# Selective attention with a top-1 expert layer: the router's logits and ranks moved to the end of a slot, one batch's logits in four column groups, ranks in two products, block ends by transfers

## The chip, the cores and the metric

The kernel runs on one core of a Trainium2 chip. The metric is the device time of one launch in microseconds (us); the median of three runs is compared. A core has five engines with instruction queues of their own: TensorE (PE; its weight loads are shown apart, as PEld), VectorE (DVE), ScalarE (ACT), GpSimd (POOL) and SyncE (SP), which here only issues transfers. Each runs its queue in order and waits on semaphores. A matmul takes a stationary operand from SBUF (the weight load) and streams a moving operand through the array into PSUM.[...]

## The reference, cut to what matters

Eight batches, eight heads, 576 tokens, 64 channels per head; then eight experts with a hidden size of 1024. All fp32.

```python
scores = scale * q @ k^T + min(-(cum[i] - cum[j]), 0)   # cum: running sum of max(s, 0); causal
attn   = softmax(scores)                                # divided by (sum + 1e-9)
x      = attn @ v                                       # (B, S, 512), heads side by side
logits = x @ w_gate                                     # eight columns
local  = sigmoid(x @ w_local)                           # one column
for b, s in order:
    fresh = argmax(logits[b, s])
    e = fresh if s == 0 or local[b, s] < 0.5 else prev_e
    prev_e = e
    p = softmax(logits[b, s])
    out[b, s] = p[e] * (relu(x[b, s] @ w1[e]) @ w2[e])
```

A token either takes its own best expert or that of the token before it, so the choice is a running scan along each batch. Tokens are then sorted by expert, so that an expert's weights meet many tokens at once.

## The kernel before

**Attention** goes in slots. There are 32 pairs (eight batches, four head pairs each), and slot n computes the scores of pair n and the values of pair n-1. In PE order a slot is: `scores` in four units (L884; 384, 2 x 192, 448 and 320 + 64 columns, each for two heads side by side in the row halves of the array), then the first block of `values` (L909, query blocks 0 to 5: 48 records in the trace), then the second block (query blocks 6 to 8: 52 records). An fp32 matmul leaves two records. Behind each block DVE takes the block out of PSUM (L915, L916), and behind the second it transposes the pair's rows into `xt` (L927, function `turn`). ACT computes the exponentials of the scores (L885), POOL masks the diagonal blocks (L870), DVE multiplies the values of a later batch by key weights (L856, `weigh`).

The rest is planned by hand into places of slots with `plan(slot, place, f)`: place 0 lies between the second and the third score unit, place 1 between the two value blocks, place 3 behind the second block, `turn` and the slot's `weigh`. What is planned into a place is issued there in the order of the `plan` calls, on whichever engines it uses.

**Router.** The eight batches make four groups of two. A group's stages are `product` (PE: x times the 9 gate columns, kept as 32 columns, into the PSUM tile `lp`; the moving operand is `xt`), `logits` (DVE: a 32 x 32 transpose `lt` and copies into `l`), `codes`, `turn1`, `turn2` (DVE: the scan over tokens, ending in the one-hot `hot` and its running count `incl`), `ranks` (PE: sums of `incl` and `hot` over partitions into the PSUM tile `pos`), `rows` (DVE: each token's row in a table in HBM), `gates` (DVE, with an index ramp by POOL: the weight p[e] beside each token) and 18 calls of `scatter` (POOL issues an indirect transfer of 128 half rows to the table). For the first three groups they lie in slots n+1 to n+12, with n = 8, 16 and 24. The last group's batches are done one by one: the product of the first in slot 29, that of the second inside the first expert unit, followed by its `codes` to `turn2`; its `ranks`, `rows`, `gates` and scatters follow there.

**PSUM.** Two banks hold the two value blocks. The other six are three tiles of two banks with one tag, `banks(name)`: each score unit takes one, and so do `lp`, `pos` and `wep`. A new tile must wait for the readers of the tile that held its banks: ACT for scores, DVE for `lp` and `pos`, ACT for `wep`.

**Single buffers.** `xt` of the even and of the odd batch of a group have one buffer each. The `turn` of the first pair of the next even batch therefore waits until the product of the group before has read it.

**Block ends.** `range_ends` and `range_ends_sum` spread the key weights at each block's end over 128 partitions into `wend`, by a mask, a selection matrix and a matmul (`wep`, L843). `wend` is read much later, in the expert phase, by a check of value ranges.

**Experts.** Work is cut into units; unit 0 starts right behind the last values. `fetch` (SP) reads a unit's rows from the table; it waits for all scatters issued before it in program order. `turn_x` (DVE) transposes them, `layer1` and `layer2` are the matmuls (L569, L593). Scatters that found no place in a slot are issued one by one between the chunks of `layer1`, and when the list of these is empty in unit 0 the units 2 and 3 are fetched. The weights of an expert are 2 MB per layer; those of the first load come in four parts, planned at place 3 of slots 25 to 28.

Of the kernel before, what the change touches and what calls it, by code (L numbers as in the profile page):

```python
# [9 lines left out]
F32 = mybir.dt.float32  # L10
# [99 lines left out]
class Router:  # L110
# [8 lines left out]
    def constants(self):  # L119
# [29 lines left out]
        self.seg = self.t("seg", [P, E, NC])  # L149
        nc.gpsimd.memset(self.seg, 1.0)  # L150
        nc.gpsimd.memset(self.seg[:, :, 0:1], 0.0)
        self.first = self.t("first", [P, P])
# [37 lines left out]

    def product(self, g, xts, banks, bs=range(GB)):

        ps = self.g.setdefault(g, {})["lp"] = banks("lp")[:, 0, : NJH * 32]
        i = 0
        for hp in range(HP):
            for d in range(2):
                for b in bs:
                    for c in range(2):
                        at = 32 * (2 * b + c)
                        j = c * (NJ - NJH)  # L200
                        self.nc.tensor.matmul(ps[at : at + 32], lhsT=self.wx[:, hp, d],  # L201
                                              rhs=xts[b][:, hp, d, j : j + NJH].rearrange("p j t -> p (j t)"),
                                              start=(i == 0), stop=(i == 2 * HP - 1))
                i += 1

    def logits(self, g, bs=range(GB)):
        v = self.nc.vector
        st = self.g[g]
        p = slice(DH * bs[0], DH * bs[-1] + DH)
        lt = self.s("lt", [P, NJH, 2, WR])  # L210
        v.transpose(lt[p].rearrange("p j q e -> p (j q e)"), st.pop("lp")[p])
        if "l" not in st:
            st["l"] = self.s("l", [P, NC, E + 1])
        l = st["l"]
        for b in bs:
            for c in range(2):
                j = b * NJ + c * NJH
                skip = c * (2 * NJH - NJ)
                for r in range(2):
                    at = 32 * (2 * b + c)  # L220
                    v.tensor_copy(l[32 * r : 32 * r + 32, j : j + NJH - skip],
                                  lt[at : at + 32, skip:, r, : E + 1])
        c = slice(bs[0] * NJ, bs[-1] * NJ + NJ)
        v.tensor_copy(l[DH:, c], l[:DH, c])
# [35 lines left out]
    def turn2(self, g):  # L260
        v = self.nc.vector
        st = self.g[g]
        for a in range(4):
# [12 lines left out]
        hot = st["hot"] = self.s("hot", deep)  # L276
        v.tensor_tensor(hot, e.unsqueeze(1).to_broadcast(deep), self.eidx.unsqueeze(2).to_broadcast(deep),
                        op=Alu.is_equal)
        incl = st["incl"] = self.s("incl", deep)
        v.tensor_tensor_scan(incl.rearrange("p e c -> p (e c)"), self.seg.rearrange("p e c -> p (e c)"),  # L280
                             hot.rearrange("p e c -> p (e c)"), 0.0, op0=Alu.mult, op1=Alu.add)

    def ranks(self, g, banks):
# [3 lines left out]
        n = E * NC  # L287
        ps = st["pos"] = banks("pos")[:, 0, : n + E]
        mm(ps[:, n:], lhsT=self.first, rhs=incl[:, :, NC - 1], start=True, stop=True)  # L289
        mm(ps[:, :n], lhsT=self.first, rhs=incl.rearrange("p e c -> p (e c)"), start=True, stop=False)  # L290
        mm(ps[:, :n], lhsT=self.later, rhs=st["hot"].rearrange("p e c -> p (e c)"), start=False, stop=True)

    def rows(self, g):
        v = self.nc.vector
        st = self.g[g]
        pos = st.pop("pos")
        n, deep = E * NC, [P, E, NC]
        at = self.s("at", deep)
        v.tensor_tensor(at, pos[:, :n].rearrange("p (e c) -> p e c", e=E), self.base.unsqueeze(2).to_broadcast(deep),
                        op=Alu.add)  # L300
        v.tensor_tensor(self.base, self.base, pos[:, n:], op=Alu.add)
        v.tensor_tensor(at, at, st["hot"], op=Alu.mult)
# [5 lines left out]
    def gates(self, g, xb):  # L308
# [3 lines left out]
        ex, hot = st.pop("ex"), st.pop("hot")  # L312
# [411 lines left out]
def attention(ctx, tc, q, k, vm, vt, s, wx, ident, recs, wend, router, experts):  # L724
# [97 lines left out]
    mask_ends = []  # L822

    def range_ends():
        mask = once.tile([B * H, NPAIR], F32, name="mask")
        nc.gpsimd.tensor_tensor(mask, ident[: B * H, :NPAIR], ident[: B * H, NPAIR : 2 * NPAIR], op=Alu.add)
        ends = once.tile([B * H, NPAIR, NJ], F32, name="ends")
        for w, a, z in ((w1, 0, 2 * G1), (w2, 2 * G1, NJ)):
            shape = [B * H, NPAIR, z - a]
            nc.vector.tensor_tensor(ends[:, :, a:z], mask.unsqueeze(2).to_broadcast(shape),  # L830
                                    w[:, a * DH + DH - 1 : z * DH : DH].unsqueeze(1).to_broadcast(shape), op=Alu.mult)
        sel = once.tile([B * H, 2, DH], F32, name="sel")
        nc.gpsimd.memset(sel, 1.0)
        nc.gpsimd.affine_select(out=sel[:, 0], in_=sel[:, 0], compare_op=Alu.is_ge, fill=0.0, base=NPAIR - 1,
                                pattern=[[0, DH]], channel_multiplier=-1)
        nc.gpsimd.affine_select(out=sel[:, 1], in_=sel[:, 1], compare_op=Alu.is_ge, fill=0.0, base=-NPAIR,
                                pattern=[[0, DH]], channel_multiplier=1)
        mask_ends.extend((sel, ends))

    def range_ends_sum():  # L840
        sel, ends = mask_ends
        wp = banks("wep")[:, 0, : NPAIR * NJ]
        mm(wp, lhsT=sel.rearrange("p h d -> p (h d)"), rhs=ends.rearrange("p n j -> p (n j)"), start=True, stop=True)  # L843
# [754 lines left out]
```

## Time and profile before

| what | us |
|---|---|
| median of three runs (752.2 to 753.45) | 752.59 |
| the profiled execution, own time | 744.71 |
| its span, first to last instruction | 743.0 |
| of it: PE busy from 7 to 218 us (attention, 211 us) | 206.81 |
| of it: PE busy from 218 to 736 us (experts, 518 us) | 518.00 |
| of it: PE busy from 736 to 743 us (last store) | 0.24 |

The granted TensorE clock is 0.998 of full speed over the span. The three PE rows come from the view that sums busy time over stretches. The profiled execution is 7.9 us shorter than the median of the timed runs; a difference between two kernels is worked out in the profiled execution's own time and then taken from the median.

The views used below are: the page's busy line and its chain of waits in shares; the chain in order of time (start, length, engine, tile, line, number of records); the groups of instructions by line and form; the waits by engine; and the timeline of one engine.

### The profile page before, as it was taken

What the parts mean: (1) busy time and instruction counts of PE and PEld (TensorE: products, weight loads), DVE (VectorE), ACT (ScalarE), POOL (GpSimd) and SP (SyncE); (2) the same over time, 40 slices, a digit from 0 to 9 for tenths busy, and PEclk for the clock granted to TensorE, in tenths of its full rate; (3) what the DMA queues carried; (4) which work ended last, traced back from release to release, by engine and by line L of the source; (5) the groups of instructions that cost most, each with busy time, mean ns of one, the idle gap of its engine ahead of it and who ended that gap; (6) DMA issues with size and microseconds to landing.
All of it is one profiled execution on the core that took longest, in us unless ns stands there. A gap on an engine that the chain in (4) does not pass through costs nothing.

```text
span 743.0 us, 15903 instructions
## 1 busy us (share of the span) xinstructions
PE 730.5 (98%) x6455; PEld 501.7 (68%) x6455; DVE 246.4 (33%) x647; ACT 162.2 (22%) x319; POOL 211.2 (28%) x453
## 2 busy tenths in 40 slices
PE   8999999999999999999999999999999999999996
PEld 5888888888786757757756376546745576647674
DVE  4655846866663741100110511230041001050110
ACT  4554544454331101101102010101100011101110
POOL 2653396686573435420110101010101001010110
PEclk9999999999999999999999999999999999999999
DMA  6672474667758958689447969996999955899000
GB/s 206 234 246 87 143 228 138 197 219 232 237 215 345 326 188 287 263 341 282 154 153 247 375 242 426 308 390 240 420 329 368 425 197 225 286 404 337 29 15 34
DMA packets 55285, 186.09 MB, mean 250 GB/s; under 512 B 11549, under 2 KB 32285, under 8 KB 46880
## 3 DMA queue, kind: packets, MB, share of 16 engines
q1 hardware_dynamic: 48400, 164.86, 62.5%
q0 software_dynamic: 6800, 20.09, 7.1%
q8 instruction: 53, 0.87, 0.5%
q14 instruction: 32, 0.26, 0.1%
HBM read 164.31 MB, written 20.88 MB: 249 GB/s over the span
## 4 chain that ended last, share of the span: by engine, by line
PE 94%; DVE 3%; POOL 0%; issue 0%; POOLq 0%
PE yp L593 35%; PE hp L569 31%; PE po L909 12%; PE ps L884 11%; PE hp L560 4%; PE lp L201 2%; DVE xb L916 0%; DVE ei L264 0%; DVE xt L927 0%; DVE recs L915 0%; POOL table L338 0%; DVE incl L280 0%; PE pos L290 0%; PE pos L289 0%; POOL e L870 0%
## 5 line engine op out<-in xcount | busy, mean ns | idle before, releaser
L593 PE MATMUL yp<-w2b,hT 128*128 128x512 f32 (+2 forms) x752 | 259.3, 594 | 0.0
L569 PE MATMUL hp<-xT,w1b 128*128 128x256 f32 (+1 forms) x1216 | 233.2, 352 | 0.0
L569 PEld LDWEIGHTS hp<-xT,w1b 128*128 128x128 f32 x1216 | 206.4, 191 | 32.5 <-issue 7.8
L593 PEld LDWEIGHTS yp<-w2b,hT 128*128 128x128 f32 (+2 forms) x752 | 108.1, 167 | 140.8 <-issue 139.5
L598 POOL DMA_INDIRECT out_dram<-y,gi x37 | 36.1, 975 | 420.4 <-DVE y L596 391.8
L571 ACT ACTIVATE hT<-hp 128x256 f32<-128x256 f32 (+1 forms) x152 | 54.0, 355 | 429.6 <-PE hp L569 429.6
L596 DVE TENSOR_SCALAR y<-yp,gi 128x512 f32<-128x512 f32 x37 | 27.6, 746 | 309.1 <-PE yp L593 302.7
L885 ACT ACTIVATE e<-ps 128x768 f32<-128x768 f32 (+1 forms) x128 | 97.1, 836 | 99.4 <-PE ps L884 99.3
L909 PE MATMUL po<-vg,e 128*64 128x66 f32 x3200 | 102.7, 224 | 1.6 <-POOL e L870 0.9
L909 PEld LDWEIGHTS po<-vg,e 128*64 128x64 f32 x3200 | 96.8, 138 | 6.1 <-POOL e L870 2.0
L884 PE MATMUL ps<-qb,kb 64*128 64x192 f32 (+4 forms) x768 | 97.5, 400 | 0.2 <-ACT e L885 0.2
L884 PEld LDWEIGHTS ps<-qb,kb 64*128 64x128 f32 x768 | 67.7, 187 | 28.6 <-ACT e L885 9.2
L338 POOL DMA_INDIRECT table<-xb,idx x72 | 73.8, 1025 | 22.3 <-issue 20.4
L870 POOL TENSOR_SCALAR_AFFINE_SELECT e<-e 128x256 f32<-128x256 f32 (+1 forms) x160 | 65.9, 438 | 45.5 <-ACT e L885 44.7
L580 DVE STREAM_TRANSPOSE hT<-hs 32x256 f32<-32x256 f32 x64 | 27.9, 436 | 74.8 <-ACT hs L562 74.0
L856 DVE TENSOR_TENSOR vg<-va,wk 128x1024 f32<-128x1024 f32 (+1 forms) x21 | 29.8, 1417 | 6.7 <-DMA va<-in_vm_dram 6.6
L916 DVE TENSOR_TENSOR xb<-po,recs 128x384 f32<-128x384 f32 x64 | 29.3, 458 | 3.0 <-DVE recs L915 0.7
L915 DVE RECIPROCAL recs<-po 128x12 f32<-128x12 f32 x64 | 13.3, 207 | 47.1 <-PE po L909 47.1
L539 DVE STREAM_TRANSPOSE xT<-xq 128x1024 f32<-128x1024 f32 (+1 forms) x23 | 23.6, 1028 | 14.9 <-DMA xq<-table 14.6
L560 PE MATMUL hp<-w1b,xT 128*32 128x512 f32 (+1 forms) x224 | 28.3, 594 | 0.0
L927 DVE STREAM_TRANSPOSE xt<-xb 128x576 f32<-128x576 f32 x32 | 24.9, 778 | 1.1
L560 PEld LDWEIGHTS hp<-w1b,xT 128*32 128x32 f32 (+1 forms) x224 | 8.2, 114 | 17.7 <-issue 17.5
(230 smaller groups left out, 171.0 us busy)
## 6 DMA issues: line engine op xcount, KB each, us to landing
w1b<-in_w_dram SPq DMA_DIRECT2D x29, 2048.0 KB, 8.2
w2b<-in_w_dram SPq DMA_DIRECT2D x29, 2048.0 KB, 15.1
kb<-in_k_dram SPq DMA_DIRECT2D x32, 288.0 KB, 3.8
qb<-in_q_dram SPq DMA_DIRECT2D x32, 288.0 KB, 3.4
xq<-table SPq DMA_DIRECT2D x56, 130.0 KB, 12.1
va<-in_vm_dram SPq DMA_DIRECT2D x7, 1024.0 KB, 7.0
w1b<-in_w_dram SPq DMA_DIRECT2D x4, 512.0 KB, 6.2
w2b<-in_w_dram SPq DMA_DIRECT2D x4, 512.0 KB
```

What stands on the lines that cost most here:

```text
L338: put = self.nc.gpsimd.indirect_dma_start(out=self.halves, in_=src, element_offset=0, in_offset=None, out_offset=bass.IndirectOffsetOnAxis ...
L560: mm(ps[d, :], lhsT=xT[:, k, d], rhs=self.ws[l][0][:, k, c * 512 : c * 512 + 512], start=(k == 0), stop=(k == DK - 1))
L569: mm(ps[:, :w], lhsT=self.ws[ls[0]][0][:, k, c * P : c * P + P], rhs=xT[:, k, :w], start=(k == 0), stop=(k == DK - 1))
L571: nc.scalar.activation(self.hT[u][:, c, :w], ps[:, :w], Act.Relu)
L593: mm(ps[d, :], lhsT=hT[:, k, n * P + d.start : n * P + d.stop], rhs=self.ws[l][1][:, k, :], start=(k == 0), stop=(k == FK - 1))
L598: put = nc.gpsimd.indirect_dma_start(out=self.out[:, :], out_offset=bass.IndirectOffsetOnAxis(ap=gi.bitcast(I32)[:, n, 0:1], axis=0), in_= ...
L856: nc.vector.tensor_tensor(vgs[b % 2][g][:, c0:c1].rearrange("p c h e -> p (c h) e")[:, :, :DH], va[:, c0:c1].rearrange("p c h e -> p (c h) ...
L870: nc.gpsimd.affine_select(out=ap, in_=ap, compare_op=Alu.is_ge, fill=0.0, base=base, pattern=n, channel_multiplier=-1)
L884: mm(ps[:, h, at : at + z - a], lhsT=kb[d, key : key + P], rhs=qb[d, a:z], start=True, stop=True)
L885: nc.scalar.activation(e, ps, Act.Exp, scale=scale)
L909: mm(po[d, j - j0, :], lhsT=weights_of(n, c, j, h), rhs=vg[:, c, 2 * hp + h, :], start=(c == 0), stop=(c == last))
L916: nc.vector.tensor_tensor(xb[:, j0:j1, :, 32 * hp : 32 * hp + 32], po[:, :, :DH].rearrange("p j (g i) -> p j g i", g=2), rec[:, :, 0].unsq ...
```

## The change

- `product` of a group of two batches keeps its four column groups; `product` of a single batch (twice, in the last group) uses four column groups of three token blocks (96 columns) where it used two of five (160 columns). The blocks of neighbouring groups overlap, and the copies of `logits` skip the overlap.
- `product` and `logits` go from place 1 to place 3 of their slot; `ranks` and `rows` from place 1 to place 3; `gates` from place 1 of slot n+4 to place 1 of slot n+5. The scatters begin at place 1 of slot n+5, where they began at place 3 of n+4, and place 0 is used in slots n+6 to n+8. The fetch of units 0 and 1 moves one slot on.
- `hot` becomes one constant tile with a 19th column of zeros for each expert; `incl` and `seg` are widened to match. Column 19 of `pos` then is the group's total, and the separate product for the totals goes.
- `range_ends` copies the block ends with POOL to a [64, 9] tile, stores it in HBM and loads it back as two broadcasts; the mask, the selection matrix, the product `wep` and ACT's copy go.

```diff
@@ -146,9 +146,11 @@
         for p in (0, DH):
             for b in range(GB):
                 nc.gpsimd.memset(self.thr[p : p + 1, b * NJ : b * NJ + 1], -1e30)
-        self.seg = self.t("seg", [P, E, NC])
+        self.seg = self.t("seg", [P, E, NC + 1])
         nc.gpsimd.memset(self.seg, 1.0)
         nc.gpsimd.memset(self.seg[:, :, 0:1], 0.0)
+        self.hot = self.t("hot", [P, E, NC + 1])
+        nc.gpsimd.memset(self.hot, 0.0)
         self.first = self.t("first", [P, P])
         nc.gpsimd.memset(self.first[:DH], 1.0)
         nc.gpsimd.memset(self.first[DH:], 0.0)
@@ -188,38 +190,38 @@
     def s(self, name, shape, dt=F32, **kw):
         return self.sb.tile(shape, dt, name=name, **kw)
 
+    @staticmethod
+    def columns(bs):
+
+        if len(bs) == 2:
+            return NJH, [(b, j, j // (NJ - NJH)) for b in bs for j in (0, NJ - NJH)]
+        return 3, [(bs[0], j, min(j, 1)) for j in range(0, NJ - 2, 2)]
+
     def product(self, g, xts, banks, bs=range(GB)):
 
-        ps = self.g.setdefault(g, {})["lp"] = banks("lp")[:, 0, : NJH * 32]
-        i = 0
-        for hp in range(HP):
-            for d in range(2):
-                for b in bs:
-                    for c in range(2):
-                        at = 32 * (2 * b + c)
-                        j = c * (NJ - NJH)
-                        self.nc.tensor.matmul(ps[at : at + 32], lhsT=self.wx[:, hp, d],
-                                              rhs=xts[b][:, hp, d, j : j + NJH].rearrange("p j t -> p (j t)"),
-                                              start=(i == 0), stop=(i == 2 * HP - 1))
-                i += 1
+        n, groups = self.columns(bs)
+        ps = self.g.setdefault(g, {})["lp"] = banks("lp")[:, 0, : n * 32]
+        last = HP * 2 - 1
+        for i in range(HP * 2):
+            hp, d = divmod(i, 2)
+            for c, (b, j, _) in enumerate(groups):
+                self.nc.tensor.matmul(ps[32 * c : 32 * c + 32], lhsT=self.wx[:, hp, d],
+                                      rhs=xts[b][:, hp, d, j : j + n].rearrange("p j t -> p (j t)"),
+                                      start=(i == 0), stop=(i == last))
 
     def logits(self, g, bs=range(GB)):
         v = self.nc.vector
         st = self.g[g]
-        p = slice(DH * bs[0], DH * bs[-1] + DH)
+        n, groups = self.columns(bs)
         lt = self.s("lt", [P, NJH, 2, WR])
-        v.transpose(lt[p].rearrange("p j q e -> p (j q e)"), st.pop("lp")[p])
+        v.transpose(lt[:, :n].rearrange("p j q e -> p (j q e)"), st.pop("lp"))
         if "l" not in st:
             st["l"] = self.s("l", [P, NC, E + 1])
         l = st["l"]
-        for b in bs:
-            for c in range(2):
-                j = b * NJ + c * NJH
-                skip = c * (2 * NJH - NJ)
-                for r in range(2):
-                    at = 32 * (2 * b + c)
-                    v.tensor_copy(l[32 * r : 32 * r + 32, j : j + NJH - skip],
-                                  lt[at : at + 32, skip:, r, : E + 1])
+        for c, (b, j, skip) in enumerate(groups):
+            for r in range(2):
+                v.tensor_copy(l[32 * r : 32 * r + 32, b * NJ + j + skip : b * NJ + j + n],
+                              lt[32 * c : 32 * c + 32, skip:n, r, : E + 1])
         c = slice(bs[0] * NJ, bs[-1] * NJ + NJ)
         v.tensor_copy(l[DH:, c], l[:DH, c])
 
@@ -273,33 +275,30 @@
         v.tensor_scalar(e, cf[:, :NC], -1.0, None, Alu.add)
         v.tensor_scalar(e, e, E - 1, None, Alu.bitwise_and)
         deep = [P, E, NC]
-        hot = st["hot"] = self.s("hot", deep)
-        v.tensor_tensor(hot, e.unsqueeze(1).to_broadcast(deep), self.eidx.unsqueeze(2).to_broadcast(deep),
-                        op=Alu.is_equal)
-        incl = st["incl"] = self.s("incl", deep)
+        v.tensor_tensor(self.hot[:, :, :NC], e.unsqueeze(1).to_broadcast(deep),
+                        self.eidx.unsqueeze(2).to_broadcast(deep), op=Alu.is_equal)
+        incl = st["incl"] = self.s("incl", [P, E, NC + 1])
         v.tensor_tensor_scan(incl.rearrange("p e c -> p (e c)"), self.seg.rearrange("p e c -> p (e c)"),
-                             hot.rearrange("p e c -> p (e c)"), 0.0, op0=Alu.mult, op1=Alu.add)
+                             self.hot.rearrange("p e c -> p (e c)"), 0.0, op0=Alu.mult, op1=Alu.add)
 
     def ranks(self, g, banks):
         mm = self.nc.tensor.matmul
         st = self.g[g]
         incl = st.pop("incl")
-        n = E * NC
-        ps = st["pos"] = banks("pos")[:, 0, : n + E]
-        mm(ps[:, n:], lhsT=self.first, rhs=incl[:, :, NC - 1], start=True, stop=True)
-        mm(ps[:, :n], lhsT=self.first, rhs=incl.rearrange("p e c -> p (e c)"), start=True, stop=False)
-        mm(ps[:, :n], lhsT=self.later, rhs=st["hot"].rearrange("p e c -> p (e c)"), start=False, stop=True)
+        ps = st["pos"] = banks("pos")[:, 0, : E * (NC + 1)]
+        mm(ps, lhsT=self.first, rhs=incl.rearrange("p e c -> p (e c)"), start=True, stop=False)
+        mm(ps, lhsT=self.later, rhs=self.hot.rearrange("p e c -> p (e c)"), start=False, stop=True)
 
     def rows(self, g):
         v = self.nc.vector
         st = self.g[g]
-        pos = st.pop("pos")
-        n, deep = E * NC, [P, E, NC]
+        pos = st.pop("pos").rearrange("p (e c) -> p e c", e=E)
+        deep = [P, E, NC]
         at = self.s("at", deep)
-        v.tensor_tensor(at, pos[:, :n].rearrange("p (e c) -> p e c", e=E), self.base.unsqueeze(2).to_broadcast(deep),
+        v.tensor_tensor(at, pos[:, :, :NC], self.base.unsqueeze(2).to_broadcast(deep),
                         op=Alu.add)
-        v.tensor_tensor(self.base, self.base, pos[:, n:], op=Alu.add)
-        v.tensor_tensor(at, at, st["hot"], op=Alu.mult)
+        v.tensor_tensor(self.base, self.base, pos[:, :, NC], op=Alu.add)
+        v.tensor_tensor(at, at, self.hot[:, :, :NC], op=Alu.mult)
         row = self.s("row", [P, NC])
         v.tensor_reduce(row, at.rearrange("p e c -> p c e"), axis=AX, op=Alu.add)
         idx = st["idx"] = self.s("idx", [P, NC], I32, bufs=2)
@@ -309,7 +308,7 @@
         v = self.nc.vector
         st = self.g[g]
         st["x"] = xb
-        ex, hot = st.pop("ex"), st.pop("hot")
+        ex, hot = st.pop("ex"), self.hot[:, :, :NC]
         for b in range(GB):
             self.nc.gpsimd.iota(xb[b].bitcast(I32)[:, :, :, XW - 2], pattern=[[DH, NJ], [0, 2]],
                                 base=(g * GB + b) * S, channel_multiplier=1)
@@ -819,29 +818,15 @@
                                       cps[d, i].rearrange("p (h b a) -> p h b a", h=2, b=B))
                 i += 1
 
-    mask_ends = []
-
     def range_ends():
-        mask = once.tile([B * H, NPAIR], F32, name="mask")
-        nc.gpsimd.tensor_tensor(mask, ident[: B * H, :NPAIR], ident[: B * H, NPAIR : 2 * NPAIR], op=Alu.add)
-        ends = once.tile([B * H, NPAIR, NJ], F32, name="ends")
+
+        ends = once.tile([B * H, NJ], F32, name="ends")
         for w, a, z in ((w1, 0, 2 * G1), (w2, 2 * G1, NJ)):
-            shape = [B * H, NPAIR, z - a]
-            nc.vector.tensor_tensor(ends[:, :, a:z], mask.unsqueeze(2).to_broadcast(shape),
-                                    w[:, a * DH + DH - 1 : z * DH : DH].unsqueeze(1).to_broadcast(shape), op=Alu.mult)
-        sel = once.tile([B * H, 2, DH], F32, name="sel")
-        nc.gpsimd.memset(sel, 1.0)
-        nc.gpsimd.affine_select(out=sel[:, 0], in_=sel[:, 0], compare_op=Alu.is_ge, fill=0.0, base=NPAIR - 1,
-                                pattern=[[0, DH]], channel_multiplier=-1)
-        nc.gpsimd.affine_select(out=sel[:, 1], in_=sel[:, 1], compare_op=Alu.is_ge, fill=0.0, base=-NPAIR,
-                                pattern=[[0, DH]], channel_multiplier=1)
-        mask_ends.extend((sel, ends))
-
-    def range_ends_sum():
-        sel, ends = mask_ends
-        wp = banks("wep")[:, 0, : NPAIR * NJ]
-        mm(wp, lhsT=sel.rearrange("p h d -> p (h d)"), rhs=ends.rearrange("p n j -> p (n j)"), start=True, stop=True)
-        nc.scalar.copy(wend, wp)
+            nc.gpsimd.tensor_copy(ends[:, a:z], w[:, a * DH + DH - 1 : z * DH : DH])
+        ends_d = nc.dram_tensor("ends", (2, NPAIR * NJ), F32, kind="Internal")
+        nc.sync.dma_start(ends_d.rearrange("h (n j) -> (h n) j", j=NJ), ends)
+        for h, d in enumerate(heads):
+            nc.sync.dma_start(wend[d], ends_d[h : h + 1].to_broadcast([DH, NPAIR * NJ]))
 
     def ones_column(b, g, c0, c1):
         to = vgs[b % 2][g][:, c0:c1].rearrange("p c h e -> p (c h) e")
@@ -936,17 +921,17 @@
 
     for g in range(NG - 1):
         n = HP * GB * (g + 1)
-        plan(n + 1, 1, lambda g=g: router.product(g, of(g), banks))
-        plan(n + 1, 1, lambda g=g: router.logits(g))
+        plan(n + 1, 3, lambda g=g: router.product(g, of(g), banks))
+        plan(n + 1, 3, lambda g=g: router.logits(g))
         plan(n + 2, 1, lambda g=g: router.codes(g))
         plan(n + 3, 1, lambda g=g: router.turn1(g))
         plan(n + 3, 3, lambda g=g: router.turn2(g))
-        plan(n + 4, 1, lambda g=g: router.ranks(g, banks))
-        plan(n + 4, 1, lambda g=g: router.rows(g))
-        plan(n + 4, 1, lambda g=g: router.gates(g, [xs[b] for b in range(g * GB, g * GB + GB)]))
-        places = [(n + 4, 3)]
-        for m in range(n + 5, n + 12):
-            if m - n in (5, 6, 7) and m < NPAIR:
+        plan(n + 4, 3, lambda g=g: router.ranks(g, banks))
+        plan(n + 4, 3, lambda g=g: router.rows(g))
+        plan(n + 5, 1, lambda g=g: router.gates(g, [xs[b] for b in range(g * GB, g * GB + GB)]))
+        places = []
+        for m in range(n + 5, n + 13):
+            if m - n in (6, 7, 8) and m < NPAIR:
                 places.append((m, 0))
             places += [(m, 1), (m, 3)] if m <= NPAIR else []
         for c in range(NC):
@@ -958,15 +943,14 @@
             plan(m, p, lambda g=g, c=c, after=after: router.scatter(g, c, after))
     plan(3, 3, router.constants)
     n = NPAIR - HP + 1
-    plan(n, 1, lambda: router.product(NG - 1, (xts[B - 2],), banks, (0,)))
-    plan(n, 1, lambda: router.logits(NG - 1, (0,)))
-    plan(5, 1, range_ends)
-    plan(6, 1, range_ends_sum)
+    plan(n, 3, lambda: router.product(NG - 1, (xts[B - 2],), banks, (0,)))
+    plan(n, 3, lambda: router.logits(NG - 1, (0,)))
+    plan(5, 3, range_ends)
     n = 2 * HP * GB
     plan(n + 7, 1, lambda: router.assign_early(0))
     for i in range(4):
         plan(n + 9 + i, 3, lambda i=i: experts.load(0, None, i))
-    plan(n + 12, 1, lambda: (experts.fetch(0), experts.fetch(1)))
+    plan(n + 13, 1, lambda: (experts.fetch(0), experts.fetch(1)))
     plan(n + 14, 1, lambda: router.assign_early(1))
     plan(n + 15, 3, lambda: experts.turn_x(0))
 
```

## The prediction

> **What bounds the kernel now.** First the page's busy line and its chain of waits in shares:
>
> ```profile
> PE 730.5 (98%) x6455; PEld 501.7 (68%) x6455; DVE 246.4 (33%) x647; ACT 162.2 (22%) x319; POOL 211.2 (28%) x453
> ...
> PE 94%; DVE 3%; POOL 0%; issue 0%; POOLq 0%
> ```
>
> TensorE is busy 98% of the span and is 94% of the chain. What the change is worth is therefore what it takes off PE's queue or adds to it; work on other engines counts only where PE waits for it. Who makes PE wait stands in the waits by engine; the three longest of a short list:
>
> ```profile
> PE pos L289 <- DVE recs L915: 2.0, 3, 0.7
> PE warm L791 <- DVE xb L767: 1.5, 1, 1.5
> PE po L909 <- POOL e L870: 0.9, 1, 0.9
> ```
>
> The first is the ranks' product: three times PE stands between two value blocks until DVE has finished `incl`. The second is the start, the third is in slot 31; the change touches neither. Next the chain in order of time, to price what lies between score and value work. An undisturbed slot, a slot with a product, and one with ranks:
>
> ```profile
> 48.32 2.95 PE ps L884 x24
> 51.28 3.07 PE po L909 x100
> 54.34 2.95 PE ps L884 x24
> ...
> 60.36 2.95 PE ps L884 x24
> 63.32 1.55 PE po L909 x48
> 64.87 2.31 PE lp L201 x64
> 67.18 1.67 PE po L909 x52
> 68.84 2.95 PE ps L884 x24
> ...
> 138.41 0.36 PE pos L289 x2
> 138.76 0.35 PE pos L290 x2
> 139.11 0.24 PE pos L291 x2
> 139.36 1.67 PE po L909 x52
> 141.02 2.95 PE ps L884 x24
> ```
>
> Scores to scores is a slot: 54.34 - 48.32 = 6.02 us bare, and 68.84 - 60.36 = 8.48 with a product. So a product costs PE 2.46 us, of which 2.31 are its own and 0.15 two more changes of shape. By the same subtraction (score starts 41.47 and 48.32, 193.74 and 202.21; for the ranks two slots each: 74.86 to 88.56, 127.14 to 141.02, 179.85 to 193.74):
>
> - `wep`, slot 6: 0.83 us
> - ranks, three in attention: 1.66, 1.84, 1.85; the fourth, in unit 0, is 0.12 + 0.35 + 0.24 = 0.71 (241.68 us). Sum 6.06
> - half product in slot 29: 2.45; in unit 0: 2.30 (223.68 us) and about 0.08 around it
>
> **The change, part by part.**
>
> *Block ends by transfers.* PE loses 0.83 us, ACT a copy of 0.40, DVE two products of 0.36, POOL 1.6 us (0.24 + 0.20 + 0.96 + 0.23). POOL gains two small strided copies (its row of 64 x 32 took 0.24) that lie in slot 5 behind the masks. SP gains three issues, two of which wait for the store; the nearest landing, kb's median, is 3.8 us. Queued behind them is the load of pair 10's q and k (issued at 44.47), which slot 10 needs at 66: 20 us of cover. `wend` is read in unit 2. Gain 0.83.
>
> *Ranks.* The 8-column product goes, the others grow from 144 to 152 columns: 0.35 + 0.24 times 152/144 is 0.62, and one change of shape about 0.03, 0.65; 0.61 in unit 0. `incl` was ready at most 0.74 us after block one, and the second block takes 1.67, so the 2.0 us of stall go. 6.06 - (3 x 0.65 + 0.61) = 3.5 gain.
>
> What is late next is PSUM. In the built program, for groups 0 and 1, `pos` takes one of the three tiles and the next slot's units go to the other two: units 0 and 2 share one, unit 3 takes that of `pos`. Unit 2 then waits for the exponential of unit 0. The timeline of a slot that begins at 88.49:
>
> ```profile
> 88.49 1.24 PE L884 MATMUL ps<-qb,kb 64*128 64x384 f32 x8
> ...
> 89.51 0.81 ACT L885 ACTIVATE e<-ps 128x768 f32<-128x768 f32 x1 [4.54 <-PE ps L884]
> ```
>
> Unit 0's exponential ends 1.02 + 0.81 = 1.83 us after its first matmul. Unit 2 is due after the 768 of 1600 columns of units 0 and 1, 2.95 x 768/1600 = 1.42. A stall of 0.4 to 0.5 us, twice: take 0.95 in all. Unit 3 then starts 3.2 us or more after `pos` begins, and DVE, which must first do the second block's L915, L916 (0.20, 0.36), `turn` (0.78) and `weigh` (1.20), has read `pos` (0.31 + 0.16) at about 3.2: no more on top if `va` is there, which it is (issued at 77.41 for slot 12, 7.0 to landing, wanted near 88). For group 2 unit 2 takes the tile of `pos`, due at 2.04, free at 2.0, since that slot has no `weigh`. Ends: nothing lost, or 0.9 each for all three.
>
> *Product and logits to the end of the slot.* PE's work is the same; one change of shape fewer, 3 x 0.07 = 0.2 gain. New is a wait: `turn` of the same slot must not overwrite `xt` before the product has read it, and behind it on DVE is `lt`, which frees `lp`, for which unit 2 of the next slot waits. From the last value matmul: product done at 2.35, `turn` issued over 0.70 (61.03 to 61.73 in DVE's timeline), `lt` 0.35, so 3.5; unit 2 is due at 2.35 + 1.42 = 3.77. Hidden by 0.25 us, three times. If not, 0.3 each; taken 0. The copies of `logits` behind it (1.8 us) end 1.4 us before DVE's next value block.
>
> *Four column groups for one batch.* Each half product goes from 32 to 64 records, each of 96 instead of 160 columns. The rows, from the groups by line (busy us, mean ns of one, idle before):
>
> ```profile
> L909 PE MATMUL po<-vg,e 128*64 128x66 f32 x3200 | 102.7, 224 | 1.6 <-POOL e L870 0.9 <-DVE vg L866 0.7
> ...
> L201 PE MATMUL lp<-xt,wx 128*32 128x160 f32 x256 | 11.9, 301 | 0.0
> L201 PEld LDWEIGHTS lp<-xt,wx 128*32 128x32 f32 x256 | 9.5, 110 | 1.4 <-issue 0.3
> ```
>
> In two groups 32 records took 2.30 us, in four 64 took 2.31: the time goes with the columns and four groups stream at once. By columns alone the half costs 2.31 x 96/160 = 1.39. But that is 22 ns from record to record, closer than any in the trace: the nearest, the value matmuls, stand at 3.07/100 = 31 ns (1.96 us). **A rule speaks against the split.** The Trainium skill, "TensorE: Matmul & The Clock Gate", Part 1, section "Wait — 56ns, not 53.3ns?", says that start to start never falls below about 25 ns however few columns there are. By it 64 x 25 = 1.60, where the columns gave 1.39. I take 1.65, a little above the floor, since `po`'s 31 ns are mostly its own columns (66 x 0.9 / 2 = 30, with 0.9 ns per column from the 160 in 144 ns). Ends 1.39 and 2.31 (if 36 ns is the pitch of the loads). Gain 2 x 0.65 = 1.3. DVE's extra four copies of 0.18 are hidden: in slot 29 by three idle microseconds, in unit 0 by the 8 us before `y`.
>
> *The constants.* POOL's 0.22 us more (`hot` cleared) lie in slot 3, where its masks come late: the third mask of the pair ends near 38.7 (37.51 + 3 x 0.41) and PE uses it near 38.75. Take 0.15 lost, ends 0 and 0.25.
>
> *Scatters and fetches.* Two scatters of group 2 move into unit 0, so units 2 and 3 are fetched after eight of them, some 3 us later than 240.12; their `turn_x` comes after 262. The fetch of units 0 and 1 (192.47 before) now stands behind group 2's first scatter. Block one of slot 29 ends at 198.25; DVE needs 0.8 for it and 1.9 for `gates`, POOL 1.0 to issue, the scatter 5.0 to land: fetch at about 207, its four issues 1.9, landing 2.9: 211.5. `turn_x(0)` stood at 215.6 and comes 0.7 earlier against these. Hidden by 3.5 us. The 2 MB load behind the fetch goes from 199.6 to about 213 and is used at 249. In slots n+5 to n+9 POOL's masks end a microsecond or more before the values that need them.
>
> **Sum.** 0.83 + 3.5 + 0.2 + 1.3 - 0.95 - 0.15 = 4.7 us, against the profiled execution's own 744.71: 740.0. The median of the timed runs is 7.9 above it, with the same work in it, so 752.6 - 4.7 = **747.9**.
>
> **Rivals.**
>
> - *The new waits for PSUM eat half* (15%). For: slack at `lp` is 0.25 us, worked out from rows with jitter of that size. Then `lp` costs 3 x 0.3, the ranks 3 x 0.9 instead of 0.95, the half products stay near 1.96: 4.7 - 0.9 - 1.75 - 0.6 = 1.45, and twice that where only some of it comes: 749.7 to 751.1. Against: ACT idles 2.9 us a slot and DVE is busy a third of the time.
> - *No change to be told* (6%): both that and half products at 2.31, so 4.7 - 0.9 - 1.75 - 1.3 = 0.75 gain, 751.8. The measurement can't tell less than 0.2% (1.5 us) from nothing.
> - *Slower* (4%): the fetch of unit 0 is late. Unit 0 starts PE's expert phase, and nothing else can run there. With the 2.9 us that these transfers took it has 3.5 us to spare; the median of that row over the run is 14.7 us to landing. With that the rows come 11.8 - 3.5 = 8.3 us late, net 752.6 - 4.7 + 8.3 = 756.2. It decides against the change from a landing of 2.9 + 3.5 + 4.7 = 11 us. Against: 14.7 belongs to transfers queued among 2 MB weight loads, and the last of these ahead of the fetch is a part of 512 KB, issued some 15 us before.
>
> **How the numbers follow.** The forecast case has 75% and its own range is 746.5 (half products at 1.39, no stall at unit 2) to 749.2 (1.96, stalls of 0.6, and one product's wait of 0.3). To leave out no more than 2 in 10 the range goes to 750.4 for the first rival and to 746.0 below. Faster by over 0.2%: 75 + 15 = 90%; same 6%; slower 4%.
>
> **What would show it.** Right: no wait of `pos` for DVE; from the scores of slot n+4 to those of n+6, for groups 0 and 1, about 13.1 us (2 x 6.02 + 0.65 + 0.45), a slot with a product at 8.4; half products near 1.65; no `wep`. The waits list then has scores waiting for ACT, about 0.45 twice. Wrong: scores waiting for DVE at slots 10, 18, 26 (the `lp` wait), a half product at 2.3, or the first `layer1` waiting for `xq`.

## The result and the profile after

| us | median | lowest | highest | runs |
|---|---|---|---|---|
| before | 752.23 | 751.91 | 753.45 | 6 |
| after | 749.00 | 748.34 | 751.67 | 6 |

The ratio is 0.9959 with a 95% interval of 0.9942 to 0.9975: 3.2 us faster, between 1.9 and 4.4. The forecast was 747.9 in a range of 746.0 to 750.4.

The profiled execution of the changed kernel is the run of 751.67 us (span 749.9), while that of the kernel before took 744.71. Taken at their word, the two would show a loss of 7 us. The page's busy line and its chain of waits in shares, after:

```profile
PE 733.6 (98%) x6509; PEld 501.5 (67%) x6509; DVE 246.8 (33%) x653; ACT 162.2 (22%) x318; POOL 209.4 (28%) x452
...
PE 95%; issue 1%; DVE 1%; POOL 1%; ACT 0%; POOLq 0%; ACTq 0%
```

PE is still the bound, and there is a share that the page before had at 0%: "issue", time in which an engine waited for nothing that the profile shows. The list of waits after says where (engine, tile and line, what it waited for: us in total, times, longest):

```profile
PE po L894 <- issue: 3.6, 10, 0.4
...
PE ps L869 <- ACT e L870: 0.8, 3, 0.3
PE lp L208 <- issue: 0.7, 2, 0.4
```

The wait of `pos` for DVE (2.0 us before) is gone, the scores wait for ACT as forecast, and none waits for DVE. But the value matmuls stop ten times and the half product of unit 0 twice with no semaphore to wait for; below such a stop is called a gap. The chain at that half product:

```profile
229.90 1.49 PE lp L208 x52
231.38 0.36 issue
231.75 0.38 PE lp L208 x6
232.12 0.38 issue
232.50 0.38 PE lp L208 x5
```

With its two gaps it takes 2.98 us here, more than in the kernel before (2.30). Two questions follow: is the sum of the prediction right where these gaps are absent, and what are they?

**The sum without gaps.** In the third set of runs below, on another chip, the changed kernel was profiled without gaps at a span of 738.4 us (run e7_after). The first profile of the kernel before, at 743.0, has none either. Of its chain in order of time (start, length, engine, tile, line, records) these are the product of the block ends in slot 6 and the half products of slot 29 and unit 0:

```profile
45.98 0.68 PE wep L843 x2
...
198.25 2.30 PE lp L201 x32
...
223.68 2.30 PE lp L201 x32
```

And of e7_after, around the ranks of group 0 and the half product of slot 29:

```profile
86.08 0.46 PE pos L289 x2
86.53 0.26 PE pos L290 x2
86.79 0.87 PE ps L869 x4
...
87.74 0.82 ACT e L870
...
88.61 1.73 PE ps L869 x12
90.33 3.07 PE po L894 x100
93.40 2.95 PE ps L869 x24
...
196.96 1.46 PE lp L208 x64
198.41 2.95 PE ps L869 x24
```

Unit 0 takes 0.87 us, ACT has its exponential done at 88.56, and only at 88.61 do units 2 and 3 (12 records) start: that is the foreseen stall. Unit 1 runs in between, off the chain. The half product takes 1.46 us, where the kernel before took 2.30; in unit 0 the two figures are the same. From score start to score start, before against after:

| step | forecast gain | measured |
|---|---|---|
| block ends (slot 6: 6.85, 6.02) | 0.83 | 0.83 |
| products (three slots: 8.48, 8.33) | 0.2 | 0.45 |
| ranks (7.67 + 7.87 + 7.87 against 3 x 6.73; in unit 0 0.71, 0.52) | 3.5 | 3.40 |
| stall of unit 2 (two slots: 6.02, 6.61) | -0.95 | -1.18 |
| half products (slot 29: 8.47, 7.52; unit 0: 2.30, 1.46) | 1.3 | 1.79 |
| constants (slots 2 to 5: 24.17, 24.08) | -0.15 | 0.09 |
| not in the sum: first slot -0.24, slot 24 -0.30, last values -0.21 | 0 | -0.75 |
| sum | 4.7 | 4.63 |

The last `y` begins at 736.28 before and 731.65 after: 4.63. In slot 24 a block of values waits for DVE, which is in the small operations of `assign_early`; at the end the values of pair 31 wait for POOL's mask 1.1 us instead of 0.9. The start differs by more between executions of one kernel: the scores of slot 2 begin at 17.55 us in e7_after and at 18.29 in e0_after.

The sum of 4.63 is closer to the forecast 4.7 than its terms are: block ends came exactly, three terms better and three worse than forecast, and the misses cancel.

### The profile page after: what moved, and what is told of

It reads as the page before. It is cut to its first block, busy times and chain, and to the rows that moved or that the text cites. A ratio compares the mean times of both kernels' runs of the same rounds, so it can differ in the third digit from the quotient of the medians.

```text
span 749.9 us, 16025 instructions
## 1 busy us (share of the span) xinstructions
PE 733.6 (98%) x6509; PEld 501.5 (67%) x6509; DVE 246.8 (33%) x653; ACT 162.2 (22%) x318; POOL 209.4 (28%) x452
## 4 chain that ended last, share of the span: by engine, by line
PE 95%; issue 1%; DVE 1%; POOL 1%; ACT 0%; POOLq 0%; ACTq 0%
PE yp L592 34%; PE hp L568 31%; PE po L894 13%; PE ps L869 12%; PE hp L559 4%; PE lp L208 1%; POOL table L337 0%; ACT e L870 0%; PE pos L289 0%; POOL e L855 0%; PE pos L290 0%; DVE y L595 0%; POOL out_dram L597 0%; DVE xb L901 0%; POOLq L93 0%
## 5 line engine op out<-in xcount | busy, mean ns | idle before, releaser
L894 PE MATMUL po<-vg,e 128*64 128x66 f32 x3200 | 106.7, 224 | 5.9 <-issue 3.6
L894 PEld LDWEIGHTS po<-vg,e 128*64 128x64 f32 x3200 | 99.2, 138 | 11.3 <-issue 7.2
L855 POOL TENSOR_SCALAR_AFFINE_SELECT e<-e 128x256 f32<-128x256 f32 (+1 forms) x160 | 64.0, 421 | 63.0 <-ACT e L870 62.2
```

Source lines behind the costliest of these rows:

```text
L855: nc.gpsimd.affine_select(out=ap, in_=ap, compare_op=Alu.is_ge, fill=0.0, base=base, pattern=n, channel_multiplier=-1)
L894: mm(po[d, j - j0, :], lhsT=weights_of(n, c, j, h), rhs=vg[:, c, 2 * hp + h, :], start=(c == 0), stop=(c == last))
```

## The experiments

Four sets of runs, each on a chip of its own with runs of the kernel before beside it (medians, us):

| set | before | kernels |
|---|---|---|
| 1 | 752.21 | e0_before 753.28, e0_after 749.25, e1_columns 752.29, e2_rows_first 748.54 |
| 2 | 745.27 | e3_scatters 740.91, e4_transfers 742.15, e5_under_scores 743.77, e6_ranks 743.71 |
| 3 | 745.17 | e7_after 741.12, e8_scatters 741.23 |
| 4 | 744.95 | e9_rows_scatters 740.11, e10_under_scores 742.80 |

So the chips are of two kinds: that of set 1 stands at 752 us, as the result does, the three others at 745, as the first profile does (744.71).

### The two kernels again: e0_before, e0_after, e7_after

No edit.

> The kernel before, unchanged, with a profile of its own beside the others of this call. Theory A (the profile of before on record, 744.7 us, is like the timed runs, only shorter by a constant): its profile has no PE gaps that no semaphore explains, its span is near 743, and the 3 us between the two kernels come from PE items alone. Theory B (PE also stops where nothing in the kernel makes it wait, in stretches where the transfer engines are full, and the profile on record happened to have none of it): the profile here has a span near 750 and several PE gaps of 0.3 to 0.5 us put down to 'issue', as the profile of after has (4.3 us in the list of waits).

> The changed kernel, unchanged, to narrow the interval and to have a second profile of it. Theory A: 4.7 us faster as in the sum, ratio 0.9938. Theory B: the PE items give about 5 us and the unexplained gaps are of the same size in both kernels, give or take 1 to 2 us from profile to profile; ratio 0.994 to 0.997, and the gaps stand at other places in this second profile than in the first.

> The changed kernel as it is, beside the kernel before. In the first set both kernels had gaps of PE in the values of slots 13 to 32; in the second set, on another chip, neither the kernel before (745.3 us) nor the changed one with seven scatters more (740.9 us) had any. If the gaps belong to the chip and both kernels have them alike, the difference of the two is that of the sum on any chip: 4.7 us (4.76 us by the chains of the second set, up to the last tile), 747.5 beside 752.2, or 740.6 beside 745.3. If the gaps eat some of the gain, it is 3 us where there are gaps (as in the first set) and 4.4 to 4.8 us where there are none.

Set 1: the kernel before, profiled again, has a span of 751.9 and six waits of `po` for "issue" (2.0 us), which its first profile has none of. Slot by slot, from score start to score start, its two profiles agree within 0.1 us in slots 2 to 12; slots 13 to 31, in which scatters are issued, are 7.8 us longer in set 1. e0_after against before: 0.996 (0.9946 to 0.9974). Set 3: e7_after against before 0.9948 (0.9934 to 0.9961), 4.05 us, and no gaps. So most of the 7 us between the chips lies in slots with gaps, in both kernels (e0_after is 6.8 us longer than e7_after in slots 13 to 31); the first profile was no sample of the timed runs. Where no gap falls, the slots of set 1 show the terms of the sum again: slot 6 goes from 6.85 to 6.02 us, slot 9 from 8.48 to 8.33, slot 29 from 8.47 to 7.52, and the stalled slots 13 and 21 stand at 6.61.

What lies at a gap? The chain of the changed kernel's first profile, in values of slot 15:

```profile
103.93 1.20 PE po L894 x36
105.13 0.21 issue
105.34 0.36 PE po L894 x4
105.71 0.40 issue
106.11 1.32 PE po L894 x33
107.42 0.39 issue
107.81 0.99 PE po L894 x25
```

and POOL's timeline there (start, length, engine, line, operation):

```profile
104.48 0.98 POOL L337 DMA_INDIRECT table<-xb,idx  x1 [0.16 <-issue]
105.47 0.77 POOL L855 TENSOR_SCALAR_AFFINE_SELECT e<-e 128x256 f32<-128x256 f32 x2
106.18 0.09 POOL L334 MEMSET gap<- 1x1 f32 x1
106.44 0.98 POOL L337 DMA_INDIRECT table<-xb,idx  x1 [0.17 <-issue]
```

Scatters end at 105.46 and 107.42; PE stops at 105.13, 105.71 and 107.42. The masks behind them are those of the next pair, so these values do not need them. In e7_after, with the same scatters at the same place, the 100 records take 3.07 us as ever. I counted value matmuls from slot 2 on that start more than 115 ns after the one before: e0_after has 19 such places and all lie within a scatter or the 0.3 us behind it (6.1 us together), e0_before 19 of 20 (6.4 of 6.7 us), e2_rows_first 22 of 22 (8.5 us), e1_columns 23 of 23. Scatters and the 0.3 us behind them fill 44 to 45% of slots 13 to 31 there, so this is not chance. In the profile of the result it is 23 of 25. The two others lie in slots 4 and 5, long before its first scatter; the earlier:

```profile
32.97 1.10 PE po L894 x36
34.08 0.20 issue
34.28 1.91 PE po L894 x57
```

The loading of code does not explain the places: transfers of the instruction queues (q8 and q14 on the page, 53 and 31 packets in the result's profile as in e7_after) overlap 3 of these 25, 5 of 20 in e0_before and 3 of 19 in e0_after, and fill 19 to 20% of the time. In the first profile of the kernel before and in e7_after there are two such places each, of which the larger one, 1.1 to 1.3 us, ends with a mask that is wanted.

### Scatters or full transfer engines: e3_scatters, e8_scatters, e4_transfers

Many gaps lie where the sixteen transfer engines are busy, so two theories stood: the scatters that POOL issues (S), or full transfer engines (D). e3 and e8, the same kernel, add scatters:

```diff
...
+    def extra(m):
+        dump = nc.dram_tensor(f"dump{m}", (P, 2 * XW), F32, kind="Internal")
+        nc.gpsimd.tensor_copy(router.gap, recs[0:1, m - 1, 0, 0:1])
+        nc.gpsimd.indirect_dma_start(out=dump[:, :], in_=router.pad, ...
...
+    for m in range(5, 12):
+        plan(m, 1, lambda m=m: extra(m))
```

e4 adds `nc.sync.dma_start(dump[:, :, :], q[m % B])` at the same places instead. (The slots called 16 and 24 in its expectation are 15 and 23 by the kernel's numbers.)

> The changed kernel with seven more scatters of 128 rows into a tensor of their own, in slots 5 to 11, each behind value block one, where the kernel has no scatters and no gaps. In the runs of the kernels so far PE stops or slows in the values of slots 13 to 32, 6 us in all, where no other engine's work is needed. Theory S (POOL's indirect transfers do it): in the profile of the changed kernel of the first set, 0.3 us is lost at the end of a scatter that lies beside values, so slots 5 to 11 go from 6.02 to about 6.3 us each, and the time rises by about 2 us over 749.2 us. Theory D (the sixteen transfer engines are full, and PE's instructions come late): seven transfers of 0.13 MB fill little, slots stay at 6.02, time within 0.5 us of 749.2.

> The same kernel as e3_scatters: seven more scatters of 128 rows in slots 5 to 11. Only a chip on which the kernel before has gaps (about 752 us) can tell anything: theory S, each costs PE about 0.3 us in its slot's values there, so 2 us over e7_after and gaps at the ends of these scatters in the profile; theory D, none in slots 5 to 11, within 0.5 us of e7_after. On a chip without gaps (745 us) both expect no difference to e7_after.

> The changed kernel with seven more plain transfers, memory to memory, of 1.1 MB each, in slots 5 to 11, issued by SP: the transfer engines are then full through these slots, without POOL. Theory D: gaps as in slots 16 and 24, which had 1.2 us each, so some 4 to 8 us more than 749.2 us. Theory S: slots stay at 6.02 us, time within 0.5 us of 749.2, unless a load of q, k or v comes late, which would show as a wait of scores or vg for it.

Both sets fell on chips without gaps, and there the seven scatters cost nothing: 740.91 and 741.23 beside 741.12, slots 5 to 11 at 6.02 us (slot 9, with its product, at 8.33). (e8's profile has one gap of 1.9 us in slot 16. It runs from 108.78 to 110.71, across two of the router's own scatters, and ends 0.2 us behind the second; it came once and is unexplained.) Whether added scatters make gaps on a chip that has them was not seen. That full engines alone make gaps is refuted without that by rows of set 1: busy time by stretches (us, then PE, PEld, DVE, ACT, POOL busy with records, granted clock, share of the transfer engines, GB/s), first e0_after in slots 2 and 3, without scatters:

```profile
23.00:29.00 6.00, 6.00 (x132) 5.09 (x128) 3.33 (x7) 3.24 (x6) 2.33 (x4) 1.00 0.95 325
```

then e0_before beside its last scatters of attention:

```profile
224.00:226.50 2.50, 1.62 (x40) 1.27 (x36) 2.00 (x4) 0.00 (x0) 1.98 (x4) 1.00 0.19 60
```

With the transfer engines 95% busy and no scatter PE has no gap in 6 us; at 19%, with scatters, it stands for 0.88 of 2.50 us at full granted clock. So nearly all gaps go with scatters. That scatters cause them, and how, is not shown, and the two gaps of the result's profile without a scatter speak against scatters as the only cause; the transfer engines were 81 to 90% busy around these two.

e4 lost 1 us for another reason, which its chain shows:

```profile
55.78 10.87 DMA va<-in_vm_dram
66.67 1.23 DVE vg L841
...
70.91 0.78 DVE xt L912
71.69 0.24 DVE lt L217
71.97 0.98 PE ps L869 x8
```

The added copies stood ahead of a load of `va`, which took 10.87 us; `weigh` came late on DVE, behind it `turn` and `lt`, and the scores of slot 10 waited for the tile of `lp`, 0.7 us; with a wait for ACT besides, the slot took 7.58 us instead of 6.02. This is the wait that the prediction kept hidden by 0.25 us: it held in e7_after, and this is what breaks it.

### The half product alone: e1_columns

The kernel before with `columns`, `product` and `logits` of the change, at their old places:

```diff
-        ps = self.g.setdefault(g, {})["lp"] = banks("lp")[:, 0, : NJH * 32]
+        n, groups = self.columns(bs)
+        ps = self.g.setdefault(g, {})["lp"] = banks("lp")[:, 0, : n * 32]
...
```

> Before, with the four column groups of 96 columns for one batch alone; everything else stays where it was. By the sum each half product goes from 2.3 to 1.65 us, 1.3 us in all. The profile of after had 1.46 us for the one in slot 29, so 0.85 there; if the second, in unit 0, is the same, 1.7 us in all (ratio 0.9977). A floor of 25 ns from record to record would show as 1.6 us or more. If the record count (32 more records per product) costs what the columns save, ratio 1.0.

The ratio is 0.9998 (0.999 to 1.0006): no gain, where set 3's profile has 1.79 us of it. The chain in slot 29:

```profile
204.14 0.94 PE lp L206 x35
205.08 0.24 issue
205.32 0.91 PE lp L206 x29
```

and POOL:

```profile
204.00 0.99 POOL L338 DMA_INDIRECT table<-xb,idx  x1 [0.17 <-issue]
```

A scatter ends at 204.99 and PE stops at 205.08. At place 1 the half product lies beside a scatter, and here its 64 records take 2.09 us; the value block behind it, also beside a scatter, takes 1.93 us instead of 1.67, so the slot stands at 8.52, as before (8.47). At place 3 of the changed kernel no scatter lies beside it, and e0_after has 1.46 on the same chip. In unit 0 the split took 1.69 plus 0.15, so the chain has a gain of 0.4 us in all. The timed runs show none; 0.4 is within their interval (up to 0.75). The split at place 1 was not run on a chip without gaps, so that the gaps eat its gain is read from one profile.

### The stall of unit 2: e2_rows_first, e9_rows_scatters

```diff
-        plan(n + 4, 3, lambda g=g: router.ranks(g, banks))
-        plan(n + 4, 3, lambda g=g: router.rows(g))
+        plan(n + 4, 2, lambda g=g: router.ranks(g, banks))
+        plan(n + 4, 2, lambda g=g: router.rows(g))
...
         values(n - 1, NJA, NJ)()
+        at(n, 2)
         turn(n - 1)
```

PE's order is unchanged (values, ranks, scores); only DVE reads `pos` ahead of `turn` and `weigh`, and so frees its tile sooner: at the ranks of group 0 it has read it 1.25 us after `pos` begins, against 2.96 us in e7_after. e9 has the seven scatters of e3 besides.

> After, with ranks and rows ahead of the turn of their slot instead of behind turn and weigh, so that DVE frees the tile of pos early and the score units keep the order of three tiles. If the wait of score unit 2 for the exponential of unit 0 comes from that tile being held, the two stalls of about 0.6 us in slots 13 and 21 go, no PE wait for ACT stays above 0.1 us, and the kernel is 1.0 us faster than after (ratio to before 0.0013 lower). If the stall has another cause, it stays.

> The changed kernel with ranks ahead of the second value block (as e2_rows_first) and the seven more scatters of e3_scatters in slots 5 to 11. On a chip without gaps (kernel before at 745 us) the seven scatters cost nothing, and this shows what the earlier ranks are worth there: the stalls of unit 2, 2 x 0.59 us, less 0.2 us of waits that stay, 740.1 us beside 741.1 for the changed kernel. On a chip with gaps (before at 752 us): theory S 748.5 + 2 = 750.5 us, with gaps in slots 5 to 11; theory D 748.5 us and no gaps there.

The chain of e2_rows_first at the ranks of group 0:

```profile
86.46 0.46 PE pos L289 x2
86.91 0.26 PE pos L290 x2
87.17 2.95 PE ps L869 x24
```

The 24 records run in 2.95 us without a stop. Set 1: 748.54, ratio 0.9946 (0.9932 to 0.9961), 0.7 us under e0_after. Set 4: 740.11, ratio 0.9937 (0.9924 to 0.9951), 1.0 us under e7_after of the set before. Both are the size of 1.18 less 0.2, but the intervals of either pair overlap; what shows the stall gone is the slot, 6.61 to 6.02 twice. It is the best version that was run.

### The ranks alone: e6_ranks

The kernel before with the ranks' part, gates and scatters of the change (`product`, `logits` and `range_ends` as before):

```diff
-        mm(ps[:, n:], lhsT=self.first, rhs=incl[:, :, NC - 1], start=True, stop=True)
...
-        plan(n + 4, 1, lambda g=g: router.ranks(g, banks))
+        plan(n + 4, 3, lambda g=g: router.ranks(g, banks))
```

> The kernel before with the ranks' part of the change alone: two products of 152 columns, ranks and rows at the end of the slot, gates and scatters behind them; products, logits and block ends as before. My sum: 6.06 - 2.56 = 3.5 us gained, less 0.95 us of stall at unit 2 and 0.15 us of constants: 2.4 us faster than before, 749.8 us. If the terms of the sum that stayed unproved in the first set (block ends 0.83, half products 1.3) are worth nothing in timed runs, all 3 us of the change lie here: 749.2 us. If the ranks' part is worth little, 751 us or more.

Measured beside 745.27: 743.71, ratio 0.9982 (0.9973 to 0.9991), 1.6 us of the 2.4 (0.7 to 2.0). Its slots 12 and 13 are 6.73 and 6.61 as in the changed kernel, but slot 20 is 7.05, slot 24 6.55 (6.27 before) and slot 29 8.65 (8.47): 0.8 us in three slots that the sum did not have. On the chain of the changed kernel, where these slots are 6.73, 6.57 and 7.52, the ranks less the stall are 2.2 of 4.63 us; the other terms of the table carry the rest.

### Scatters beside scores: e5_under_scores, e10_under_scores

On top of e2_rows_first:

```diff
-            places += [(m, 1), (m, 3)] if m <= NPAIR else []
+            places += [(m, 3), (m, 3)] if m <= NPAIR else []
```

> The changed kernel with ranks ahead of the slot's second value block (748.5 us in the first set), and each scatter that stood between the two value blocks moved to the end of the slot, so that it is issued beside the next slot's scores, whose instructions are longer. Nothing else changes. Theory S: of the 6 us that slots 13 to 32 take more than their items, 3 to 5 go: 743.5 to 745.5 us. Theory D: the transfers are the same and so are the gaps: 748.5 within 0.7 us.

> The same kernel as e5_under_scores, whose scatters are issued beside scores. On a chip without gaps it took 743.8 us, since POOL's masks came late behind two scatters. On a chip with gaps: theory S, the gaps of PE beside values go and the late masks stay, so 744 to 745.5 us, where the kernel with ranks ahead took 748.5 us; theory D, gaps and late masks both, 751 us or more.

743.77 and 742.80. The second is 2.7 us slower than e9_rows_scatters in the same set. The list of waits of e10_under_scores:

```profile
PE po L894 <- POOL e L855: 3.1, 4, 1.4
```

e9 has 1.0 here, once. Two scatters in a row stand ahead of the next pair's masks on POOL, and the values wait for these. On a chip with gaps it was not run, so this neither supports nor weakens S; where there are none the order is a loss.

## Why the prediction was right

- *PE as the bound, and the stalls that go:* right. Both named waits went or came as said, and 3.40 us of ranks stand against 3.5. The two products of a group take 0.72 in attention, not 0.65: the first of them shows 0.46 on the chain, where it had 0.35.
- *The stall of unit 2:* right in place, cause and number of times; 0.59 instead of 0.4 to 0.5 each. The working had the exponential end at 1.83 us and unit 2 due at 1.42, by its share of columns. On the chain unit 2 starts at 88.61 - 86.79 = 1.82; but units 2 and 3 take 1.73 of the 2.95 us, so that unit 2 is due at 1.22.
- *Half products:* right in kind, too small in size (1.3 for 1.79). I took 1.65 us, just above the floor that the Trainium skill states ("TensorE: Matmul & The Clock Gate", Part 1, "Wait — 56ns, not 53.3ns?": about 25 ns from start to start, by which 1.60 for 64 is an estimate). Measured were 1.46 us for 64 records in both places of e7_after, 22.8 ns each; the floor does not hold for these records in four column groups, and the columns alone, 1.39, were nearer. That the working found no records closer than 31 ns was a reading of averages. The starts of single records in the trace before already go 7, 129, 7, 129 ns in slot 29 (sets of two, 136 ns for 160 columns, and the sets of four of a group's product take 136 too); in e7_after they go 7, 6, 7, 63 (sets of four, 83 ns for 96 columns). The columns set the time of a set, and within it records start 6 to 7 ns apart. In set 1 the gain is not the same everywhere: 1.68 us in unit 0 of e0_after, 2.98 in the result's profile.
- *Block ends:* exact. *Products:* 0.15 each rather than 0.07. *Constants:* their price did not come. Nothing in the sum stood for the start, slot 24 and the last values, -0.75 us together.
- *Fetch of unit 0, the slower rival:* no wait of `xq` for it on the chain; with it the rival of a late fetch falls. The rival of new PSUM waits did not eat half: scores wait for DVE behind a product nowhere in e7_after or the result's profile, and once in e0_after (0.5 us; slot 26 takes 6.78 instead of 6.02), so the 0.25 us of cover do not always hold.
- *The step that failed* is the last: "The median of the timed runs is 7.9 above it, with the same work in it, so 752.6 - 4.7 = 747.9". The work was the same, but not PE's pace: most of the 7.9 us is PE stopped or slowed in the slots with scatters, on chips of one kind, and that part need not be alike in two kernels that place their scatters differently. On chips without gaps the gain is 4.05 us (2.9 to 4.9) in timed runs and 4.63 on the chain; on those with gaps 3.2 (1.9 to 4.4) and 3.0 (2.0 to 4.1). From profile to profile the gaps come to 6 to 9 us, and the result's own profile loses 0.68 us at the half product of unit 0 instead of gaining. So a part of the gain may go there, but it is not settled: the intervals overlap. Even without gaps the median of the timed runs stays 0.6 us under the chain, within its interval. That the total lay within 1.1 us of the forecast is in part luck: too little was put down for products and half products, and nothing for the slots that lost.

## What to carry over

Ask of a profiled execution whether it is one of the timed runs: where it is faster than all of them, find what it lacks before a difference is carried over. When a wait is taken away by moving an operation, follow the buffer that the operation now takes, to the next to use it: here half a microsecond came back at a place that could be named, and reading the tile earlier (e2) took it away without touching PE's order. The split into more and shorter matmuls paid what the columns say where PE ran without gaps (1.46 us), and not beside a scatter in set 1 (2.09 us): measure it at the place where it is to stand.

## What was not expected of the hardware

- Two kinds of chip differ by 7 us on the same program: 752.2 against 745.0 to 745.3. On the slower kind PE has gaps, most of 0.2 to 0.5 us, nearly all within or just behind POOL's indirect transfers, seen among values and half products (31 and 22.8 ns from record to record on average). Scores, which take 2.95 us for 24 records, show none. The cause is open.
- Records of 96 columns in four column groups start every 22.8 ns on average (64 in 1.46 us), in sets of four with starts 6 to 7 ns apart.
- A row of 0.98 us for a scatter on POOL (slot 15, the result's profile and e7_after) is the same on both kinds of chip; only PE beside it differs.
